# Last key block and corner of an attention output: from plain fp32 products to rounded ones, with the probabilities' way through DRAM cut in four

## The chip, the core and the metric

The kernel runs on one core of a Trainium2 chip. The metric is the device time of one execution in microseconds, as the median of the runs shown. The profile is of one execution by itself; it says when each instruction of each engine began and how long it took. The engines are TensorE (PE, with its weight loads listed apart as PEld), VectorE (DVE), ScalarE (ACT), GpSimd (POOL), and SyncE (SP), which here issues nearly all DMAs. L605 is line 605 of the kernel.

## What is computed

Causal attention with a decay for 4 x 8 heads of 576 tokens and 64 columns, then two MLPs over all 2304 tokens.

```python
def _attn_ref(q, k, v, f):                      # (4, 8, 576, 64)
    scores = scale * np.matmul(q, k.transpose(0, 1, 3, 2))
    log_f = np.log(np.clip(f, 0.0001, 1.0))
    cum = np.cumsum(log_f, axis=-1)
    decay = cum[:, :, :, None] - cum[:, :, None, :]
    scores = np.where(causal, -1000000000.0, scores + decay)
    ...
    attn = attn / (np.sum(attn, axis=-1, keepdims=True) + 1e-09)
    return np.matmul(attn, v)

x = attn_out.transpose(0, 2, 1, 3).reshape(2304, 512)
h = np.maximum(x @ w_in, 0.0);  x = (h * h) @ w_out
h = x @ w_in2;                  out = (h - np.tanh(h)) @ w_out2
```

## The kernel before

**Rounded products.** TensorE multiplies the type F32R in one pass, and plain F32 in two (the profile lists 32 instructions for the 16 products of L602). Where precision matters, the kernel splits a number into a rounded high part and the rest as a low part (`rounded`, `rest`) and adds up three products: high x high, low x high, high x low. The first MLP does so for each of its tiles of 288 tokens (`hp` at L164, `yp` at L193, twelve products of a step in a row), and so do the scores (`s_ps`).

**Stages.** Heads 0 to 7 run first, their second half beside the first MLP tile. Heads 8 to 15, here the early heads, run beside tiles 0 and 1 in pieces that `attention` issues. Heads 16 to 31, the late heads, run beside tiles 2 to 5: `plan_head` puts each step of a head into a numbered half step of the MLP, 7.75 of them from one head to the next. Behind them come the last two tiles and the second MLP. Each engine's instructions stand in one order: that of a first build up to tile 2, and the order in which the code emits them from there.

**One head.** The scores go through a row minimum (DVE, L497), an exponential (ACT, L506) and a division by the sum (POOL, L517). The probabilities `P[t]` must then be turned, keys to partitions. Early heads turn them on PE (`trans`, bank `t_ps`), where ACT rounds the high part into `PTh` and DVE writes the low part to `PTl`. Late heads turn them in 32x32 pieces on DVE (`turn`, into `T`), and the pieces get to their partitions by way of DRAM: `put` stores the whole of `T` in one DMA to `p_d`, `get` reads it back into `PTl` in four, one for each set of 32 partitions. In the next head's slots ACT rounds `PTl` to `PTh` in four steps, one per key block (`p_high`), and DVE leaves the rest in `PTl` (`p_low`).

**The output of a head** (`pv_parts`). `o_ps` holds 64 columns of V's high part times the probabilities in its lower half and V's low part in its upper half: the weights `VH[:, c]` have both, 128 columns. A product per key block and part of the probabilities: `(hi, 0)` to `(hi, 3)` and `(lo, 0)` to `(lo, 3)`. I call the first group of a late head its high block (`pv_begin`), the second its low block (`pv_end`); an MLP step stands between. Two pieces are plain F32, with raw V as weights (`VR`): the last key block of 64 keys, which only the last 128 queries see (`po4`, L602), and the corner, the first 64 queries with their own 64 keys (`corner`, L609, into a bank of its own).

```python
seq = [(hi, 0), (hi, 1), (hi, 2), (hi, 3), (None, 4), (lo, 1), (lo, 2), (lo, 3), (lo, 0)]
...
nc.tensor.matmul(po4, vr[0:rows, 4], p4, start=False, stop=False)
```

In a late head the 64 keys of the last block and the corner lie in places of `T` that causality leaves free: column block 2, piece 0, and column block 3, piece 0. They pass through `PTl` without being rounded.

**The queue on SP.** It goes in order; an instruction that waits holds up all behind it. In a late head: `put`, in every second head the two stores of x (`x_d`, L489 and L490), `get`, then the loads of the next queries and keys (`R`, `QB`) and of V (`VR`, two buffers).

## Time and profile before

| | |
|---|---|
| median of 3 runs | 1013.88 us (1013.79 to 1014.28) |
| the profiled execution | 1015.15 us, of which the span of the program is 1013.4 |
| PE busy | 990.9 us, 98% |
| weight loads (PEld) | 930.6 us, 92% |
| DVE, ACT, POOL busy | 706.9, 608.6, 381.3 us (70%, 60%, 38%) |
| heads 8 to 15 | about 140 to 253 us of the span |
| heads 16 to 31 | about 253 to 523 us |

Busy time of PE is to be read with care: a product counts as busy from its start to its modelled end, overlaps with the next one, and counts on while it stands for an operand. What a product takes from PE's time is the distance from its start to the next one's.

### The profile page before, as it was taken

What the parts mean: (1) busy time and instruction counts of PE and PEld (TensorE: products, weight loads), DVE (VectorE), ACT (ScalarE), POOL (GpSimd) and SP (SyncE); (2) the same over time, 40 slices, a digit from 0 to 9 for tenths busy, and PEclk for the clock granted to TensorE, in tenths of its full rate; (3) what the DMA queues carried; (4) which work ended last, traced back from release to release, by engine and by line L of the source; (5) the groups of instructions that cost most, each with busy time, mean ns of one, the idle gap of its engine ahead of it and who ended that gap; (6) DMA issues with size and microseconds to landing.
All of it is one profiled execution on the core that took longest, in us unless ns stands there. A gap on an engine that the chain in (4) does not pass through costs nothing.

```text
span 1013.4 us, 19745 instructions
## 1 busy us (share of the span) xinstructions
PE 990.9 (98%) x7120; PEld 930.6 (92%) x7120; DVE 706.9 (70%) x1675; ACT 608.6 (60%) x1347; POOL 381.3 (38%) x453
## 2 busy tenths in 40 slices
PE   7979999999999999999999999999999999999998
PEld 7767678888999899998999999999999999999998
DVE  5886675777676777675825668477777787877851
ACT  4886676766776667676746777456556553333330
POOL 3453455555543324343402456247456520000000
PEclk8999999999999999999999999999999999999999
DMA  8545542223556556665547984997776699434451
GB/s 265 233 139 189 182 155 81 98 80 112 213 217 230 203 209 208 224 219 187 196 150 250 357 290 172 367 381 254 282 271 249 235 343 343 147 118 135 139 167 63
DMA packets 84529, 211.54 MB, mean 209 GB/s; under 512 B 8440, under 2 KB 33072, under 8 KB 80080
## 3 DMA queue, kind: packets, MB, share of 16 engines
q1 hardware_dynamic: 84304, 210.28, 59.2%
q8 instruction: 56, 0.92, 0.4%
q14 instruction: 41, 0.34, 0.1%
q10 hardware_dynamic: 128, 0.01, 0.0%
HBM read 132.20 MB, written 78.05 MB: 207 GB/s over the span
## 4 chain that ended last, share of the span: by engine, by line
PE 77%; DMA 8%; DVE 6%; ACT 3%; issue 2%; POOL 2%; SPq 1%; DVEq 0%; ACTq 0%; POOLq 0%
PE yp L193 17%; PE hp L164 17%; PE wp L1270 16%; PE wp L1194 11%; PE o_ps L605 4%; PE wp L1282 2%; DMA raw<-in_w_dram 2%; DMA R<-in_qk_dram 2%; DMA g_d<-gq 2%; PE o_ps L406 1%; DMA PTl<-p_d 1%; DVE wt L966 1%; PE s_ps L698 1%; PE t_ps L541 1%; PE s_ps L697 1%
## 5 line engine op out<-in xcount | busy, mean ns | idle before, releaser
L164 PE MATMUL hp<-xhl,w 128*128 128x288 f32 x1536 | 236.3, 299 | 2.5 <-POOL xhl L122 1.0
L164 PEld LDWEIGHTS hp<-xhl,w 128*128 128x128 f32 x1536 | 213.1, 189 | 7.8 <-issue 1.8
L193 PE MATMUL yp<-gh,w 128*128 128x288 f32 x1024 | 212.8, 299 | 0.0
L193 PEld LDWEIGHTS yp<-gh,w 128*128 128x128 f32 x1024 | 164.4, 188 | 3.1 <-issue 2.1
L1194 PE MATMUL wp<-xo,wg 128*128 128x288 f32 x1152 | 159.9, 296 | 2.0 <-DVE gq L1201 1.9
L1270 PE MATMUL wp<-go,wg 128*128 128x256 f32 x1344 | 161.4, 283 | 0.0
L1270 PEld LDWEIGHTS wp<-go,wg 128*128 128x128 f32 x1344 | 161.4, 192 | 0.0
L1194 PEld LDWEIGHTS wp<-xo,wg 128*128 128x128 f32 x1152 | 155.0, 188 | 3.5 <-DVE gq L1201 3.4
L193 PE MATMUL yp<-gl,w 128*128 128x288 f32 x512 | 151.5, 297 | 0.0
L517 POOL TENSOR_SCALAR P<-P,ST 128x448 f32<-128x448 f32 (+4 forms) x120 | 83.4, 704 | 136.6 <-DVE ST L713 83.0
L109 ACT ACTIVATE go<-gt 128x1792 fp32r<-128x1792 f32 (+1 forms) x34 | 58.3, 1717 | 101.2 <-PE wp L1270 79.9
L497 DVE CUSTOM_DVE_ANT_0 P<-s_ps,mk 128x320 f32<-128x320 f32 (+3 forms) x151 | 63.5, 438 | 72.6 <-PE s_ps L698 41.5
L506 ACT ACTIVATE P<-P,ST 128x320 f32<-128x320 f32 (+4 forms) x151 | 84.8, 562 | 47.3 <-DVE ST L497 45.2
L193 PEld LDWEIGHTS yp<-gl,w 128*128 128x128 f32 x512 | 96.4, 188 | 0.8 <-issue 0.8
L122 DVE TENSOR_TENSOR gl<-tmp,gh 128x288 fp32r<-128x288 f32 x96 | 58.6, 611 | 51.6 <-ACT tmp L174 51.1
L122 DVE TENSOR_TENSOR go<-gt,go 128x1792 fp32r<-128x1792 f32 (+1 forms) x34 | 69.6, 2048 | 34.9 <-ACT go L109 32.0
L170 ACT ACTIVATE tmp<-hp 128x288 f32<-128x288 f32 x128 | 52.0, 406 | 63.1 <-PE hp L164 62.2
L122 POOL TENSOR_TENSOR wt<-wt,whi 128x512 f32<-128x512 f32 (+1 forms) x48 | 60.7, 1286 | 59.2 <-ACT whi L109 28.8
L174 ACT ACTIVATE tmp<-tmp 128x288 f32<-128x288 f32 x128 | 56.7, 443 | 3.4
L173 ACT ACTIVATE gh<-tmp 128x288 fp32r<-128x288 f32 x128 | 56.1, 438 | 1.9
L1201 DVE TENSOR_TENSOR gq<-wp,sm 128x288 f32<-128x288 f32 x96 | 40.8, 453 | 17.0 <-ACT sm L1200 11.3
L1245 DVE TENSOR_TENSOR gt<-gt 128x256 f32<-128x256 f32 x128 | 49.4, 428 | 1.5 <-DMA gt<-g_d 0.4
(171 smaller groups left out, 1673.7 us busy)
## 6 DMA issues: line engine op xcount, KB each, us to landing
wg<-wg_d SPq DMA_DIRECT2D x24, 896.0 KB
g_d<-gq SPq DMA_DIRECT2D x32, 576.0 KB
raw<-in_w_dram SPq DMA_DIRECT2D x16, 1024.0 KB
p_d<-T SPq DMA_DIRECT2D x16, 1024.0 KB
PTl<-p_d SPq DMA_DIRECT2D x64, 256.0 KB
raw<-in_w_dram SPq DMA_DIRECT2D x32, 512.0 KB
gt<-g_d SPq DMA_DIRECT2D x32, 512.0 KB
R<-in_qk_dram SPq DMA_DIRECT2D x24, 576.0 KB
```

The source lines that it names most:

```text
L109: eng.activation(out, in_, AF.Copy)
L122: eng.tensor_tensor(out, in_, hi.bitcast(F32), ALU.subtract)
L164: nc.tensor.matmul(ps, w[:, k * 128:(k + 1) * 128], x[:, k], start=(jj == 0), stop=(jj == 11))
L170: nc.scalar.activation(tmp, ps, AF.Relu)
L173: nc.scalar.activation(gh, tmp, AF.Square)
L174: nc.scalar.activation(tmp, tmp, AF.Square)
L193: nc.tensor.matmul(yp[m][:, :n], w[:, c], x, start=(at == 0 and j == 0), stop=(at == NF - 1 and j == 2))
L497: nc.vector.tensor_tensor_reduce(p[:rows, a:b], ps[:rows, :b - a], mk[:rows, o:o + b - a], -0.125, 3.0e38 if mn is None else mn, ALU.add, ...
L506: nc.scalar.activation(p[:rows, :n], p[:rows, :n], AF.Exp, bias=mn, scale=-1.0, accum_out=st[:rows, 1, t:t + 1])
L517: by(n_by).tensor_scalar(p[:rows, :n], p[:rows, :n], st[:rows, 3, t:t + 1], 1.0, ALU.mult, ALU.mult)
L1194: nc.tensor.matmul(ps, wg[:, ws, k * 128:(k + 1) * 128], xo[:, xs, k], start=(i == 0 and first_), stop=(i == 5), skip_group_check=True)
L1270: nc.tensor.matmul(ps, wg[:, ws, m * 128:(m + 1) * 128], YO[n][xs][:, YX[xn]], start=(j == 0 and m == 0 and i == 0), stop=(j == 2 and i == ...
```

## The change

The last key block becomes two rounded products, `(hi, 4)` and `(lo, 4)`, and the corner three (high x high, V's low part x high, high x low). For that V's fifth block is rounded too (`VH` has 5 blocks, and `VR` is only read by that rounding, so it has one buffer; the load of V moves behind the rounding in `attention`). The pieces of probabilities that lay in `PTl` raw are now split as well: `p_high(2)`, `p_low(2)` start at piece 0 and `p_high(3)`, `p_low(3)` at piece 1 instead of 2 (`LOW`). In early heads two DVE copies out of `t_ps` become one ACT and one DVE step of 64x192. `put` becomes four stores of a quarter each; each of the loads of `get` reads one quarter. `get` moves one half step ahead, from o + 7 to behind o + 6, and so ahead of the x stores. Left out of the diff: every second one of heads 0 to 7 keeps its V in the buffer of `VH`, since `VR` has one buffer now, and the table of engines (the new ACT step `pth3` as `pth` before).

```diff
@@ -62,6 +62,7 @@
 DIRECT = ((0, 6), (0, 7), (1, 6), (1, 7))
 HOME_G = {6: 0, 7: 1, 0: 2, 1: 3, 2: 4, 3: 5, 4: 6, 5: 7}
 YSEQ = (0, 6, 1, 7, 2, 3, 4, 5)
+LOW = (0, 0, 0, 1)
 PT_SZ = (64, 256, 384, 512, 576)
 
 
...
@@ -285,14 +286,15 @@
         by(pre(u) + "st").memset(ST[u], 1.0)
 
     def load_v(u):
-        VR[u] = two.tile([128, 5, D], F32, tag="VR", bufs=2, name="VR")
+        VR[u] = two.tile([128, 5, D], F32, tag="VR", bufs=1, name="VR")
         src = v[u] if u < UT else v[u].rearrange("(b i) c d -> i b (c d)", b=4)
         nc.sync.dma_start(VR[u], src)
 
     def prep_v(u):
-        VH[u] = one.tile([128, 4, 2, D], F32R, tag="VH", name="VH")
-        rounded(by(pre(u) + "vh"), VH[u][:, :, 0], VR[u][:, 0:4])
-        rest(by(pre(u) + "vl"), VH[u][:, :, 1], VR[u][:, 0:4], VH[u][:, :, 0])
+        VH[u] = one.tile([128, 5, 2, D], F32R, tag="VH", name="VH")
+        vr = VR.pop(u)
+        rounded(by(pre(u) + "vh"), VH[u][:, :, 0], vr)
+        rest(by(pre(u) + "vl"), VH[u][:, :, 1], vr, VH[u][:, :, 0])
 
 
     A_RAW, A_V, A_QA, A_QB = {}, {}, {}, {}
...
@@ -546,15 +551,14 @@
         rounded(nc.scalar, PTh[:, :nch, t - 1], src)
         rest(nc.vector, PTl[:, :nch, t - 1], src, PTh[:, :nch, t - 1])
         if t == 1:
-            rounded(by("ptr"), PT["t"][0:64, :, 3, 1], ps[0:64, 256:384].rearrange("p (q j) -> p q j", q=4))
-            rounded(by("ptr"), PT["t"][0:64, 2:4, 3, 0], ps[0:64, 384:448].rearrange("p (q j) -> p q j", q=2))
-
-
+            eh, el = (x[0:64, 3].rearrange("p t j -> p (t j)")[:, :192] for x in (PTh, PTl))
+            rounded(nc.scalar, eh, ps[0:64, 256:448])
+            rest(nc.vector, el, ps[0:64, 256:448], eh)
 
     def turn(t):
         p, T = P[t], PT["t"]
         if t == 0:
-            nc.vector.transpose(T[0:64, 0:2, 3, 0], p[0:64, :64].rearrange("p (b j) -> p b j", b=2))
+            nc.vector.transpose(T[0:64, 0:2, 3, 1], p[0:64, :64].rearrange("p (b j) -> p b j", b=2))
             return
         nch = min(t + 1, 4)
         nc.vector.transpose(T[:, :, :nch, t - 1].rearrange("p b a j -> p a b j"),
...
@@ -563,7 +567,8 @@
             nc.vector.transpose(T[:, 0:2, 2, 0], p[:, 512:576].rearrange("p (b j) -> p b j", b=2))
 
     def put(u):
-        by("put").dma_start(p_d[u % 2], PT["t"].rearrange("p b a s j -> p (b a s j)"))
+        for b in range(4):
+            by("put").dma_start(p_d[u % 2][:, 512 * b:512 * b + 512], PT["t"][:, b].rearrange("p a s j -> p (a s j)"))
 
     def get(u):
         src = p_d[u % 2].rearrange("(q i) (b n) -> i q b n", q=4, b=4)
...
@@ -572,41 +577,38 @@
             by("get").dma_start(dst.bitcast(F32), src[:, :, b])
 
     def pv_parts(u):
-        vh, vr = VH.pop(u), VR.pop(u)
+        vh = VH.pop(u)
         b, h = divmod(u, H)
         e = h % 2
         ps = bank(u, "o_ps")
         if u < UT:
             hi, lo = (PT[k].rearrange("p q a s j -> p (q a s j)").rearrange("p (c t j) -> p c t j", c=4, t=4) for k in "hl")
             po = ps.rearrange("p (s j) -> p s j", s=4)
-            at = lambda p, c, t: p[:, c, t:]
+            at = lambda p, c, t: p[0:64, 3, 0] if c == 4 else p[:, c, t:]
+            po_at = lambda t: po[:, t:]
+            p0 = lambda p: p[0:64, 3, 1, :64]
             rows = 64
-            po4, p4 = ps[0:64, 384:512].rearrange("p (q j) -> p q j", q=4), PT["t"][0:64, :, 3, 1]
-            po_at = lambda t: po[:, t:]
-            p0 = PT["t"][0:64, 2:4, 3, 0]
+            seq = [(hi, 0), (hi, 1), (lo, 1), (hi, 2), (lo, 2), (hi, 4), (hi, 3), (lo, 3), (lo, 4), (lo, 0)]
         else:
             hi, lo = PT["h"], PT["l"]
             po = ps.rearrange("p (q s j) -> p q s j", q=4, s=4)
-            at = lambda p, c, t: p[:, :, c, t:]
+            at = lambda p, c, t: p[:, :, 2, 0] if c == 4 else p[:, :, c, t:]
+            po_at = lambda t: po[:, :, t:]
+            p0 = lambda p: p[:, 0:2, 3, 1]
             rows = 128
-            po4, p4 = po[0:64, :, 3], lo[:, :, 2, 0].bitcast(F32)
-            po_at = lambda t: po[:, :, t:]
-            p0 = lo[:, 0:2, 3, 0].bitcast(F32)
-        seq = [(hi, 0), (hi, 1), (lo, 1), (hi, 2), (lo, 2), (hi, 3), (lo, 3), (None, 4), (lo, 0)]
-        if u >= UT:
-            seq = [(hi, 0), (hi, 1), (hi, 2), (hi, 3), (None, 4), (lo, 1), (lo, 2), (lo, 3), (lo, 0)]
+            seq = [(hi, 0), (hi, 1), (hi, 2), (hi, 3), (hi, 4), (lo, 1), (lo, 2), (lo, 3), (lo, 4), (lo, 0)]
+        po4 = po[:, 3] if u < UT else po[:, :, 3]
 
         def products(a, z):
             for n, (pt, c) in list(enumerate(seq))[a:z]:
-                if pt is None:
-                    nc.tensor.matmul(po4, vr[0:rows, 4], p4, start=False, stop=False)
-                    continue
                 t = max(0, c - 1)
-                nc.tensor.matmul(po_at(t), vh[:, c].rearrange("p a d -> p (a d)"), at(pt, c, t), start=(n == 0), stop=(n == 8))
+                w, o = (vh[0:rows, c], po4) if c == 4 else (vh[:, c], po_at(t))
+                nc.tensor.matmul(o, w.rearrange("p a d -> p (a d)"), at(pt, c, t), start=(n == 0), stop=(n == len(seq) - 1))
 
         def corner():
             ps0 = PS0[u] = bank(u, "o0_ps")
-            nc.tensor.matmul(ps0[0:64, 0:64], vr[0:rows, 0], p0, start=True, stop=True)
+            for n, (a, p) in enumerate(((0, hi), (1, hi), (0, lo))):
+                nc.tensor.matmul(ps0[0:64, 0:64], vh[0:rows, 0, a], p0(p), start=(n == 0), stop=(n == 2))
 
         xt = one.tile([64, 512], F32, tag="xsh", name="xt")
 
...
@@ -636,7 +638,7 @@
 
     def pv(u):
         products, corner, upper, out = pv_parts(u)
-        products(0, 9)
+        products(0, 10)
         corner()
         upper()
         out()
...
@@ -653,8 +655,6 @@
 
     def attention(u0):
         for p in range(u0 - 2, UT):
-            if u0 - 1 <= p:
-                load_v(p + 1)
             for t in (1, 4, 3, 2):
                 if p >= u0:
                     trans(p, t)
...
@@ -670,12 +670,13 @@
                     prep(p + 2)
                 if t == 3 and p >= u0:
                     prep_v(p)
+                if t == 3 and u0 - 1 <= p:
+                    load_v(p + 1)
             if p + 3 < NU:
                 load(p + 3)
             if p >= u0:
                 pv(p)
             if p + 1 == UT:
-                nc.gpsimd.memset(PT["t"][0:64, 2:4, 3, 0], 0.0)
                 turn(1)
                 turn(0)
                 put(UT)
...
@@ -716,11 +717,11 @@
         normalise(P[t], ST[u], t, f"{pre(u)}n{t}")
 
     def p_high(c):
-        s0 = max(0, c - 1)
-        rounded(by("pth"), PT["h"][:, :, c, s0:], PT["l"][:, :, c, s0:].bitcast(F32))
+        s0 = LOW[c]
+        rounded(by("pth3" if c == 3 else "pth"), PT["h"][:, :, c, s0:], PT["l"][:, :, c, s0:].bitcast(F32))
 
     def p_low(c):
-        s0 = max(0, c - 1)
+        s0 = LOW[c]
         lo = PT["l"][:, :, c, s0:]
         rest(by(f"ptl{c}"), lo, lo.bitcast(F32), PT["h"][:, :, c, s0:])
 
...
@@ -745,7 +746,7 @@
         PV[u][0](0, 5)
 
     def pv_end(u):
-        PV[u][0](5, 9)
+        PV[u][0](5, 10)
         PV[u][1]()
 
     def plan(slot, f, *a, behind=False):
...
@@ -795,7 +796,7 @@
             plan(o + 5, turn, 1)
             plan(o + 5, turn, 0)
             plan(o + 5, put, k)
-            plan(o + 7, get, k)
+            plan(o + 6, get, k, behind=True)
         if k == UT + 1:
             plan(o, prep_v, UT)
         if k + 1 < NU:
```

The products of late head 18 on **PE**, `o_ps<-PTh` the high block and `o_ps<-PTl` the low block, with the MLP step (`yp`) between. Before:

```order
L605 MATMUL o_ps<-PTh,VH 128x512 x2
L605 MATMUL o_ps<-PTh,VH 128x4x96
L605 MATMUL o_ps<-PTh,VH 128x4x64
L602 MATMUL o_ps<-PTl,VR 64x4x32
...
L605 MATMUL o_ps<-PTl,VH 128x512
L605 MATMUL o_ps<-PTl,VH 128x4x96
L605 MATMUL o_ps<-PTl,VH 128x4x64
L605 MATMUL o_ps<-PTl,VH 128x512
L609 MATMUL o_ps<-PTl,VR 64x64
```

and with the change (its lines are 1 or more further down):

```order
L606 MATMUL o_ps<-PTh,VH 128x512 x2
L606 MATMUL o_ps<-PTh,VH 128x4x96
L606 MATMUL o_ps<-PTh,VH 128x4x64
L606 MATMUL o_ps<-PTh,VH 128x4x32
...
L606 MATMUL o_ps<-PTl,VH 128x512
L606 MATMUL o_ps<-PTl,VH 128x4x96
L606 MATMUL o_ps<-PTl,VH 128x4x64
L606 MATMUL o_ps<-PTl,VH 128x4x32
L606 MATMUL o_ps<-PTl,VH 128x512
L611 MATMUL o_ps<-PTh,VH 64x64 x2
L611 MATMUL o_ps<-PTl,VH 64x64
```

The rows that read `VR` (F32, 64 columns of weights, each two passes on the chip) are gone; one product over 4x32 columns stands at the end of the high block and one in the low block, and three of 64 columns behind the low block.

The same stretch of heads on the **SP queue**, two heads in a row, the first with x stores behind its predecessor's output. Before:

```order
L566 DMA p_d_83<-T 128x2048
L489 DMA x_d_81<-xsh 128x576
L490 DMA x_d_81<-xs 128x576
L572 DMA PTl<-p_d_83 32x4x512 x4
L269 DMA R<-in_qk_dram 128x1152
L271 DMA QB<-aug_d 4x1152
L290 DMA VR<-in_v_dram 128x1x320
L566 DMA p_d_84<-T 128x2048
L572 DMA PTl<-p_d_84 32x4x512 x4
```

and with the change:

```order
L571 DMA p_d_83<-T 128x512 x4
L577 DMA PTl<-p_d_83 32x4x512 x4
L494 DMA x_d_81<-xsh 128x576
L495 DMA x_d_81<-xs 128x576
L270 DMA R<-in_qk_dram 128x1152
L272 DMA QB<-aug_d 4x1152
L291 DMA VR<-in_v_dram 128x1x320
L571 DMA p_d_84<-T 128x512 x4
L577 DMA PTl<-p_d_84 32x4x512 x4
```

One store of 2048 columns became four of 512, and the four loads stand right behind them, ahead of the two x stores; the loads of R, QB and VR kept their places behind.

## Rows read from the trace of the kernel before

**Rows 1.** The page: busy time of each engine and its share of the span.

```profile
PE 990.9 (98%) x7120; PEld 930.6 (92%) x7120; DVE 706.9 (70%) x1675; ACT 608.6 (60%) x1347; POOL 381.3 (38%) x453
```

**Rows 2.** Waits of PE: engine, line, releaser: total us, times, longest.

```profile
PE o_ps L605 <- issue: 0.9, 1, 0.9
```

**Rows 3.** Timeline of PE, head 16: start us, us, engine, line, operation.

```profile
266.40 0.91 PE L605 MATMUL o_ps<-PTh,VH 128*128 128x512 f32 x4
267.24 0.43 PE L602 MATMUL o_ps<-PTl,VR 128*64 128x128 f32 x2
267.60 1.85 PE L164 MATMUL hp<-xhl,w 128*128 128x288 f32 x12
269.29 0.92 PE L605 MATMUL o_ps<-PTl,VH 128*128 128x512 f32 x4
270.13 0.33 PE L609 MATMUL o_ps<-PTl,VR 128*64 128x64 f32 x2
270.39 0.53 PE L193 MATMUL yp<-gh,w 128*128 128x288 f32 x2
270.76 0.30 PE L193 MATMUL yp<-gl,w 128*128 128x288 f32 x1
```

**Rows 4.** The same timeline, twelve MLP products with rounded products around them.

```profile
259.05 1.75 PE L164 MATMUL hp<-xhl,w 128*128 128x288 f32 x12
260.64 0.31 PE L697 MATMUL s_ps<-QA 128*128 128x320 f32 x1
```

**Rows 5.** Timeline of PE, an early head.

```profile
224.87 0.28 PE L605 MATMUL o_ps<-PTh,VH 128*128 128x256 f32 x1
224.99 0.28 PE L605 MATMUL o_ps<-PTl,VH 128*128 128x256 f32 x1
225.20 0.43 PE L602 MATMUL o_ps<-T,VR 64*64 64x128 f32 x2
225.56 0.50 PE L605 MATMUL o_ps<-PTl,VH 128*128 128x512 f32 x1
```

**Rows 6.** Timeline of PE, rounded score products over 64 columns.

```profile
261.13 0.21 PE L697 MATMUL s_ps<-QA 128*128 128x64 f32 x1
261.18 0.28 PE L698 MATMUL s_ps<-QB 68*128 68x64 f32 x1
```

**Rows 7.** Timeline of the weight loads beside them.

```profile
261.04 0.19 PEld L697 LDWEIGHTS s_ps<-QA 128*128 128x128 f32 x1
261.16 0.19 PEld L698 LDWEIGHTS s_ps<-QB 68*128 68x128 f32 x1
```

**Rows 8.** Timeline of the SP queue: stores and loads of turned probabilities.

```profile
318.31 0.33 SPq L566 DMA_DIRECT2D p_d<-T  x1
...
324.25 2.54 SPq L572 DMA_DIRECT2D PTl<-p_d  x4
...
335.88 0.32 SPq L566 DMA_DIRECT2D p_d<-T  x1
340.06 2.53 SPq L572 DMA_DIRECT2D PTl<-p_d  x4
```

**Rows 9.** Lines by form, ScalarE: busy us, mean ns, idle before and releaser.

```profile
L109 ACT ACTIVATE PTh<-PTl 128x512 fp32r<-128x512 f32 x32 | 18.4, 623 | 16.7 <-DMA PTl<-p_d 16.7
...
L109 ACT ACTIVATE PTh<-PTl 128x256 fp32r<-128x256 f32 x16 | 6.4, 403 | 0.0
```

**Rows 10.** Timeline of ScalarE, one head: idle before in brackets.

```profile
348.17 1.87 ACT L109 ACTIVATE PTh<-PTl 128x512 fp32r<-128x512 f32 x4 [1.47 <-DMA PTl<-p_d]
```

**Rows 11.** Busy time of the instructions on o_ps in 16 windows, one per high block.

```profile
266.00:268.60 2.60, 1.27 (x6) 0.89 (x6) 0.00 (x0) 0.00 (x0) 1.00 0.07 25
...
348.50:351.80 3.30, 1.89 (x6) 0.94 (x6) 0.00 (x0) 0.00 (x0) 1.00 0.47 170
...
sum 48.30, PE 24.97 PEld 14.61 DVE 0.00 ACT 0.00; mean PE 1.56 PEld 0.91 DVE 0.00 ACT 0.00
```

**Rows 12.** Busy time of all engines, clock, DMA share and GB/s, one stretch.

```profile
319.00:321.50 2.50, 2.50 (x18) 2.14 (x17) 1.58 (x3) 1.06 (x3) 2.10 (x3) 1.00 1.01 413
```

More of the change, by code (lines that the diff above doesn't have):

```diff
@@ L330, in first @@
             r = (one if tag == "R" else two).tile([128, 2, S], F32, tag=tag, name="R0")
-            vr = two.tile([128, 5, D], F32, tag="VR", bufs=2, name="VR")
+            if h % 2:
+                vr = one.tile([128, 5, 2, D], F32, tag="VH", name="V0").rearrange("p c a d -> p (c a d)")[:, :5 * D].rearrange("p (c d) -> p c d", c=5)
+            else:
+                vr = two.tile([128, 5, D], F32, tag="VR", bufs=1, name="VR")
             nc.sync.dma_start(r[0:64], qk[h][0:64])
```

2 rows, old and new, of the table ENG are left out of this document.

## The prediction

> **What bounds the kernel now.** I read the page's engine line first: TensorE (PE) is busy for 98% of the span, and the weight loads for 92% [rows 1]. So a microsecond of PE work that goes away is a microsecond of time, wherever PE isn't standing for somebody else. The list of PE's waits holds little, 0.9 us as its largest before the attention's last products [rows 2], but a product that stands for its operand counts as busy, so busy time hides the rest. The timeline of PE by start times therefore decides: the distance from one start to the next is what a product costs.
>
> **The late heads (16 to 31).** In one of them [rows 3] PE runs four rounded products on the high parts (266.40), two passes of the plain fp32 product of the last key block (267.24), one step of the MLP, four rounded products on the low parts (269.29), two passes of the plain fp32 corner (270.13), and goes on. The fp32 block takes 267.24 to 267.60 = 0.36 us, the corner 270.13 to 270.39 = 0.26 us. Around them lies a second cost, which the durations don't tell. The twelve products behind the fp32 block take 267.60 to 269.29 = 1.69 us, where twelve undisturbed ones take 259.05 to 260.64 = 1.59 us [rows 4]: 0.10 us to leave fp32. Likewise the two products behind the corner take 270.39 to 270.76 = 0.37 us against 2 x 0.133 = 0.27: 0.10 again. Entering costs about as much: in an early head [rows 5] one product over 256 columns takes 0.12 us (224.87 to 224.99) and the next one, alike but with fp32 behind it, 0.21 (to 225.20): 0.09 us. There the fp32 block takes 225.20 to 225.56, the same 0.36.
>
> So each head pays for the block 0.09 + 0.36 + 0.10 = 0.55 us and for the corner 0.09 + 0.26 + 0.10 = 0.45, together **1.00 us**; I take the early heads' exits and corner as the late ones'.
>
> **What takes their place on PE.** Five rounded products: high and low part of the last block (128 columns of probabilities, 128 of weights) and three corner products (64 and 64). No such product is in the trace. The nearest rows are the rounded score products over 64 columns [rows 6]: from one to the next 0.05 us. But the weight loads beside them, of 128 columns, start 0.12 us apart [rows 7], so a stream of such products goes at the pace of its loads. I price a product by the load it must leave room for: 0.11 where the next load has 128 columns (between the 0.12 here and the 0.10 that the exposed first load costs behind fp32), and half, 0.06, where it has 64, an estimate. Late heads: 0.11 + 0.11 + 0.06 + 0.06 + 0.11 = 0.45; early heads, where the third corner product stands apart: 0.11 + 0.11 + 0.06 + 0.11 + 0.11 = 0.50. Net per head: 0.55 (16 late ones) and 0.50 (8 early ones): 8.8 + 4.0 = **12.8 us** off PE. Bounds: all five at 0.05 gives 0.75 x 24 = 18.0; all five at the 0.133 of a product over 288 columns gives (1.00 - 0.665) x 24 = 8.0. I stay near the middle, since the loads' row is of the nearest shape.
>
> The Trainium skill (TensorE: Matmul & The Clock Gate, LDWEIGHTS) puts a weight load at its columns over 1.2, which is 107 ns for 128 columns and 53 for 64: the trace's 0.12 agrees, and no row here shows the other alone. The same page (Back-to-back issue gap) gives about 81 ns for a load and product of 128 columns in a stream; by that the two wide products would be 0.03 us cheaper each, an estimate of 24 x 0.06 = 1.4 us more gain.
>
> **The store and load of turned probabilities.** A late head's probabilities go out as one store of 1 MB and come back as four loads. Without attention stores in between, the loads stand from 335.88 to 340.06 for the store to land, 4.18 us; in every second head the two x stores stand ahead of them, and they go out at 324.25, 5.9 us after the store of 318.31 [rows 8]. They land late: ScalarE stands idle for them for 16.7 us in all [rows 9]. In one head it waits 1.47 us, goes at 348.17 into the four rounding steps [rows 10], and PE follows product by product. The table of PE's time in the 16 high blocks [rows 11] sums that up: an undisturbed one has 1.27 us, the one behind 348.17 has 1.89, and eight of the 16 have 1.67 or more. Sixteen undisturbed ones would have 20.3, the sum is 24.97: 4.6 us of standing inside the blocks, and the 0.9 of [rows 2] ahead of one of them. Together **5.5 us**.
>
> After the change the loads need only their own quarter, and PTl free (PE's corner of the head before). The whole store's data flow for the 2.5 us from 319.0 to 321.5 [rows 12]; a quarter has 0.6, so the first should land 4.18 - 1.9 = 2.3 us after its issue, and the others follow about as fast as the loads can be issued (0.63 each). Loads start 1.9 us earlier in the heads without stores and, standing ahead of the stores now, 3.6 earlier in the others. The head at 348.17 waited 1.47, so it is covered. ScalarE's rounding gets longer: pieces of 384 and 256 columns become 512 and 384, together 623 - 403 = 0.22 us per head [rows 9], and the low parts on VectorE by about as much. Where the loads are early this lies under the MLP step ahead of the block; if that cover is gone it costs 0.22 x 16 = 3.5 us. I count 5.0 of the 5.5 us as won. Ends: nothing, and 5.5.
>
> **Other edits.** In the early heads two VectorE copies become one ScalarE and one VectorE step of 64x192, and V's fifth block is rounded too. ScalarE's nearest row is 0.40 us [rows 9]; PE reads these late in its block, so MLP products hide it; shown uncovered it would be 0.40 x 8 = 3.2 us. I charge 0.5. One V buffer less: the load of V now stands behind the rounding of the V before, on the SP queue ahead of the query/key load R; a head is 17 us long (318.31 to 335.88), V is needed one head later, so I charge nothing. Behind the earlier loads wait the x stores, by at most 4 x 0.63 = 2.5 us, and they feed an MLP tile that comes much later. The part before the early heads and all behind the last head keep their order.
>
> **Sum.** -12.8 - 5.0 + 0.5 = -17.3 us. The profiled execution took 1015.15 us (span 1013.4 and 1.75 around it), 1.27 above the median of 1013.88. 1015.15 - 17.3 = 997.85, less 1.27: **996.6 us**.
>
> **Rivals.**
> - *The stalls stay* (18%). The quarters or PTl's release hold the loads back, or ScalarE comes late for its own reasons. For it: PE gets faster, so each load has less time. Against it: 1.9 and 3.6 us of lead. 996.6 + 5.0 = 1001.6.
> - *The small products are dear* (12%): 0.133 each. 996.6 + 4.8 = 1001.4. For it: none of this shape is in the trace. Against: 0.05 at 64 columns.
> - *The freed PE time is swallowed* (6%): VectorE and ScalarE, both longer now, set the pace in part; half of 12.8 is lost: 1003.0. Against: they are busy for 70% and 60% [rows 1].
> - *Slower: the four quarter stores land one after the other* (4%). If each paid the whole store's time but for its data, 4.18 - 1.9 = 2.3 us in turn, the last lands after 9.2. The last load now goes out at 340.06 + 1.9 = 341.96; then at 335.88 + 9.2 = 345.1, 3.1 us later, and in the other heads at 327.5 instead of 326.1, 1.4 later. 8 x 3.1 + 8 x 1.4 = 36 us of lateness; the 8 heads without a stall today can hide perhaps 1.5 each (my choice), 12, so 24 us are added: 1013.88 - 12.3 + 24 = 1025.6. It decides once the lateness beyond that cover passes 12.3 us, about 1.5 us in each head. For it: the four loads of a quarter take from 340.06 to 348.17, 8.1 us, twice as long as the whole store. Against: the store alone fills the DMA engines at 413 GB/s [rows 12], and nothing in the rows makes one quarter wait for another. The Trainium skill (DMA: Bandwidth & Descriptors, Rules for kernel authors) speaks for this rival: coalesce small transfers, 1 MiB and more for bandwidth, since each has a fixed part of about 2.0 us. By the page's fit a quarter takes 2.6 us, an estimate; four in turn would be 10.4, and no row shows whether they go in turn.
> - *No change worth measuring* (3%): the time between PE's parts is filled again.
>
> **How the numbers follow.** The forecast's own case has 57%. The rivals that still gain (36%) lie at 1001 to 1003; the lower end is both terms at their best, 1013.88 - 18.0 - 5.5 + 0.5 = 990.9. The range 990 to 1003 leaves out the slower and the neutral case and what is beyond the bounds. Faster by over 0.2% (2 us, about what can be told here): 0.93; within it: 0.03; slower: 0.04.
>
> **What would show it.** On PE: no fp32 passes in heads 8 to 31, five short products of 0.05 to 0.13 us, and no 0.1 us loss behind them. The 16 high blocks, now five products each: near 0.95 us plus the drain, without the stalled half. On SP: the first load some 2.3 us after the first quarter store. On ScalarE: the 16.7 us of waiting for PTl down to a few. It is wrong if PE's distances between starts shrink and the time doesn't, or if ScalarE still stands for PTl.

## The result

The changed kernel takes 1004.42 us (median of 4 runs, 1003.81 to 1005.74), the kernel before 1014.08 beside it (4 runs, 1013.79 to 1015.37): a ratio of 0.9904, 95% interval 0.9887 to 0.9921. The profiled execution took 1004.15 us, its span is 1002.4, so 11.0 less than before where 17.3 were forecast. PE's busy time on the page is 979.8 us, 11.1 less than in [rows 1], and by itself that says nothing about where. Three marks cut the span: PE's 64x64 turn, which each of the early heads 8 to 15 has once, the start of head 16's high block, and the first product of the second MLP.

**The early heads lost time.** PE's 64x64 transposes, before and after (of each group: duration, then start of its first and last):

```profile
L544 PE MATMUL t_ps<-ident,P x8: 242/243/244, 143.9 to 240.6; 64*64 64x64 f32 x8
```

```profile
L549 PE MATMUL t_ps<-ident,P x8: 242/243/244, 142.9 to 242.0; 64*64 64x64 f32 x8
```

From the first to the last of the eight, seven heads, it was 96.7 us and is 99.1 now: 2.4 longer. Head 16's high block starts at 269.00, where before it was 266.40 [rows 3]: 2.6 later, and 3.5 earlier was forecast.

**The late heads gained what was forecast.** PE's timeline in head 16, as [rows 3] had it (start, length, instructions):

```profile
269.00 0.98 PE L606 MATMUL o_ps<-PTh,VH 128*128 128x512 f32 x5
269.82 1.81 PE L165 MATMUL hp<-xhl,w 128*128 128x288 f32 x12
271.46 1.03 PE L606 MATMUL o_ps<-PTl,VH 128*128 128x512 f32 x5
272.33 0.25 PE L611 MATMUL o_ps<-PTh,VH 128*64 128x64 f32 x2
...
272.47 0.51 PE L194 MATMUL yp<-gh,w 128*128 128x288 f32 x2
272.82 0.30 PE L194 MATMUL yp<-gl,w 128*128 128x288 f32 x1
```

The fp32 pieces are gone. The four high products with the fp32 block, and the twelve MLP products behind it, took 266.40 to 269.29 = 2.89 us; the five high products and the same twelve take 269.00 to 271.46 = 2.46; the low ones, the corner and the two MLP products behind it took 269.29 to 270.76 = 1.47 and take 271.46 to 272.82 = 1.36. That is 0.54 us a head, and 0.55 was forecast.

The stalls in the high blocks are gone too, but for one (the 16 windows, as [rows 11]):

```profile
268.60:270.40 1.80, 0.98 (x5) 0.87 (x5) 0.00 (x0) 0.00 (x0) 1.00 0.00 0
...
347.50:350.00 2.50, 1.54 (x5) 0.86 (x5) 0.00 (x0) 0.00 (x0) 1.00 0.43 155
...
sum 27.80, PE 16.24 PEld 13.98 DVE 0.00 ACT 0.00; mean PE 1.01 PEld 0.87 DVE 0.00 ACT 0.00
```

Undisturbed blocks have 0.97 to 0.99, the one of head 21 has 1.54: the sum is 0.6 over 16 times 0.98, where before it was 4.6 over. ScalarE's wait for the low tile fell from the 16.7 us of [rows 9] to 1.8:

```profile
L110 ACT ACTIVATE PTh<-PTl 128x512 fp32r<-128x512 f32 x48 | 26.6, 621 | 2.8 <-DMA PTl<-p_d 1.8 <-issue 1.0
```

The SP queue, as [rows 8], shows why (start, us, instructions):

```profile
270.40 1.79 SPq L571 DMA_DIRECT2D p_d<-T  x4
272.71 2.97 SPq L577 DMA_DIRECT2D PTl<-p_d  x4
...
318.77 2.48 SPq L571 DMA_DIRECT2D p_d<-T  x4
321.45 2.99 SPq L577 DMA_DIRECT2D PTl<-p_d  x4
324.49 0.58 SPq L494 DMA_DIRECT2D x_d<-xsh  x1
```

The first load goes out 2.31 us after the first quarter store (270.40 to 272.71), and 2.68 in the other head shown, where 2.3 was forecast; over the late heads it is 2.2 to 3.6, mostly 2.2 to 2.3. The x stores now stand behind the four loads (324.49).

**Behind attention** nothing changed. The first rounded product of the second MLP and the first of its last part (L1194 and L1270 before, one line lower after), before and after:

```profile
L1270 PE MATMUL wp<-go,wg x1344: 280/283/283, 825.2 to 986.3; 128*128 128x256 f32 x192
L1194 PE MATMUL wp<-xo,wg x1152: 288/294/402, 642.9 to 824.2; 128*128 128x288 f32 x192
```

```profile
L1271 PE MATMUL wp<-go,wg x1344: 280/283/284, 814.2 to 975.3; 128*128 128x256 f32 x192
L1195 PE MATMUL wp<-xo,wg x1152: 288/294/403, 632.1 to 813.2; 128*128 128x288 f32 x192
```

It starts at 632.1 in place of 642.9, and takes 182.1 us to its last part in place of 182.3. The balance: +2.6 to head 16, then 363.1 us to the second MLP in place of 376.5, -13.4, and -0.2 behind it: -11.0, the difference of the spans.

### The profile page after: what moved, and what is told of

It reads as the page before. It is cut to its first block, busy times and chain, and to the rows that moved or that the text cites. A ratio compares the mean times of both kernels' runs of the same rounds, so it can differ in the third digit from the quotient of the medians.

```text
span 1002.4 us, 19872 instructions
## 1 busy us (share of the span) xinstructions
PE 979.8 (98%) x7144; PEld 931.6 (93%) x7144; DVE 717.1 (72%) x1667; ACT 612.4 (61%) x1355; POOL 393.1 (39%) x452
## 4 chain that ended last, share of the span: by engine, by line
PE 80%; DVE 7%; DMA 5%; ACT 3%; issue 2%; POOL 1%; SPq 1%; DVEq 0%; POOLq 0%; ACTq 0%
PE hp L165 18%; PE yp L194 17%; PE wp L1271 16%; PE wp L1195 13%; PE o_ps L606 4%; PE wp L1283 2%; PE o_ps L411 2%; DMA raw<-in_w_dram 1%; DVE wt L967 1%; PE s_ps L699 1%; DMA g_d<-gq 1%; PE t_ps L546 1%; PE s_ps L698 1%; PE t_ps L392 1%; DVE P L502 1%
## 5 line engine op out<-in xcount | busy, mean ns | idle before, releaser
L522 POOL TENSOR_SCALAR P<-P,ST 128x448 f32<-128x448 f32 (+4 forms) x120 | 93.9, 790 | 137.8 <-DVE ST L714 77.5
L1333 POOL TENSOR_TENSOR gq<-sm,sm 128x288 f32<-128x288 f32 x32 | 28.5, 892 | 55.7 <-ACT sm L1332 34.6
```

Source lines behind the costliest of these rows:

```text
L522: by(n_by).tensor_scalar(p[:rows, :n], p[:rows, :n], st[:rows, 3, t:t + 1], 1.0, ALU.mult, ALU.mult)
```

## The experiments

The table holds all of them, as the text below reads them. "Early" is the time from the first to the last of the eight turns, "late" from head 16's high block to the second MLP, "second MLP" as above; these three are from one profiled execution each, the ratio from the timed ones. Each ratio is to the kernel before as it was timed beside that row's kernel; its medians there lay between 1014.08 and 1015.51 us, so medians of different rows can differ by a microsecond or two for that reason alone.

| kernel | median us (range; runs) | ratio to before, 95% | early | late | second MLP |
|---|---|---|---|---|---|
| before | 1013.88 (1013.79 to 1014.28; 3) | | 96.7 | 376.5 | 182.3 |
| after | 1004.42 (1003.81 to 1005.74; 4) | 0.9904 (0.9887 to 0.9921) | 99.1 | 363.1 | 182.1 |
| after, again | 1006.82 (1005.08 to 1008.06; 6) | 0.9909 (0.9875 to 0.9942) | 99.2 | 362.5 | 185.2 |
| 128 rows | 1004.06 (999.38 to 1006.26; 4) | 0.9889 (0.9857 to 0.9921) | 94.6 | 363.1 | 185.2 |
| 128 rows, again | 1003.29 (999.46 to 1005.56; 6) | 0.9869 (0.9835 to 0.9903) | 94.3 | 362.1 | 183.3 |
| adjacent | 1005.48 (1001.2 to 1008.56; 4) | 0.9906 (0.9874 to 0.9939) | 97.4 | 363.0 | 184.6 |
| 128 rows for the turn too | 1002.6 (999.1 to 1006.45; 5) | 0.9869 (0.9846 to 0.9892) | 94.9 | 362.0 | 187.0 |
| late heads on 64 rows | 1020.95 (1018.19 to 1027.24; 8) | 1.0047 (1.002 to 1.0075) | 100.8 | 376.8 | 185.9 |
| late part only | 1005.85 (1003.46 to 1009.49; 6) | 0.9903 (0.9869 to 0.9937) | 98.8 | 362.3 | 183.8 |
| products alone | 1016.58 (1012.88 to 1021.29; 10) | 1.0022 (1.0003 to 1.0042) | 98.6 | 372.9 | 186.1 |
| transfers alone | 1013.01 (1007.82 to 1015.7; 10) | 0.9961 (0.9931 to 0.9991) | 97.2 | 370.4 | 185.6 |
| whole store, early loads | 1008.03 (1005.13 to 1013.67; 10) | 0.9935 (0.9909 to 0.9962) | 99.2 | 366.2 | 182.6 |
| quarters, late loads | 1011.15 (1008.13 to 1014.78; 10) | 0.9962 (0.9945 to 0.9979) | 99.2 | 369.5 | 182.3 |

**How to read it.** The second MLP takes 182.1 to 187.0 us from one execution to another, with no order by kernel. Its largest group of waits on PE, in after and in the same kernel once more (total, times, longest):

```profile
PE wp L1195 <- DVE gq L1202: 1.6, 2, 1.4
```

```profile
PE wp L1195 <- DVE gq L1202: 3.6, 5, 1.7
```

So two medians some 3 us apart can hardly be told apart. The stretches are steadier: of the six executions with the early heads of after, five have 98.6 to 99.2 us for them (the sixth 100.8), and the late stretch of a kernel profiled twice differs by 0.6 and 1.0. I read those, and the medians where they agree.

### What the early heads lost

In after, one early head on PE, and behind it the same stretch of the kernel before:

```profile
197.77 0.73 PE L606 MATMUL o_ps<-PTh,VH 128*128 128x512 f32 x2
198.43 0.30 PE L611 MATMUL o_ps<-PTh,VH 64*64 64x64 f32 x2
...
198.72 0.40 PE L165 MATMUL hp<-xhl,w 128*128 128x288 f32 x1
...
199.19 0.34 PE L606 MATMUL o_ps<-PTh,VH 128*128 128x384 f32 x1
199.38 0.34 PE L606 MATMUL o_ps<-PTl,VH 128*128 128x384 f32 x1
199.65 0.64 PE L606 MATMUL o_ps<-PTh,VH 64*128 64x128 f32 x2
200.12 0.96 PE L606 MATMUL o_ps<-PTl,VH 128*128 128x256 f32 x3
200.92 0.55 PE L165 MATMUL hp<-xhl,w 128*128 128x288 f32 x3
```

```profile
197.04 0.73 PE L605 MATMUL o_ps<-PTh,VH 128*128 128x512 f32 x2
...
197.96 0.67 PE L164 MATMUL hp<-xhl,w 128*128 128x288 f32 x3
...
200.07 1.09 PE L164 MATMUL hp<-xhl,w 128*128 128x288 f32 x7
```

From the first product to the end of the block it takes 197.77 to 200.92 = 3.15 us with one MLP product inside; before it was 197.04 to 200.07 = 3.03 with three. Less 0.133 for each of these: 3.02 against 2.63. The head has lost 0.39 us, where the forecast had 0.50 won; read in the same way, the eight early heads lose 0.37 to 0.58 each. In the rows of after the products with `64*128` and `64*64` stand out. The one over 384 columns ahead of the first takes 199.38 to 199.65 = 0.27 (its neighbour, alike but with 128 rows behind it, 0.19); and 199.65 to 200.12, a 64-row product and one over 256 columns, is 0.47.

**Theory:** a product over 64 rows between products over 128 rows costs TensorE a switch on the way in and one on the way out. **Rivals:** the products stand for operands that come late; a narrow product is dear by itself; the V buffers.

**128 rows.** The early heads' small products over all 128 rows; rows 64 to 127 of the probabilities are zeros, written once, so the result stays.

```diff
-            at = lambda p, c, t: p[0:64, 3, 0] if c == 4 else p[:, c, t:]
-            p0 = lambda p: p[0:64, 3, 1, :64]
-            rows = 64
+            at = lambda p, c, t: p[:, 3, 0] if c == 4 else p[:, c, t:]
+            p0 = lambda p: p[:, 3, 1, :64]
+            rows = 128
```

Expected:

> The changed kernel, but the early heads' last-block and corner products run over 128 rows in place of 64 (rows 64 to 127 of the probabilities are zeros written once, so the result is the same). Theory (a product over 64 rows between products over 128 rows costs TensorE about 0.1 us on the way in and 0.1 on the way out, as the trace of after has it: 0.45 for each of two, and about 0.49 for the corner): each last-block product falls to about 0.11 to 0.12 and the corner to about 0.23, 0.9 us a head over 8 heads, so 1004.4 - 7 = 997.5 us (996 to 999.5). Rival 1 (the products stand for probabilities that ScalarE and VectorE round late): no change, 1004.4, and the products keep 0.25 us. Rival 2 (a product over 128 columns alone among wider ones is dear whatever its rows): no change, 1004.4. Rival 3 (the loss sits in the loads of V): no change on the whole, though the products become cheap.

And timed once more, beside the changed kernel itself:

> The changed kernel once more, beside its variants on one chip. Both theories: 1004.4 us by the runs so far; the executions of the kernel before spread from 1012.5 to 1017.7 on this chip, so the median here may lie 1 to 2 us away from it. The stretch of the early heads, from the first MLP products of head 8's steady part to those of head 16, should again be longer than in the kernel before, by 1 to 2 us.

> The changed kernel with the early heads' last-block and corner products over 128 rows, timed beside the changed kernel itself. In its first look PE reached the end of the early heads 5.1 us earlier than in the changed kernel, and 4.1 us of that stood at the end of attention. Theory (the row switch is what the early heads lost by): 4 us below the changed kernel of the same call, 1000.4 if that stands at 1004.4. Rival (the last projection fills the time again, by a wait of its own): within 1 us of the changed kernel.

The same head of the second of them:

```profile
195.84 0.73 PE L606 MATMUL o_ps<-PTh,VH 128*128 128x512 f32 x2
196.41 0.25 PE L611 MATMUL o_ps<-PTh,VH 128*64 128x64 f32 x2
...
196.56 0.38 PE L165 MATMUL hp<-xhl,w 128*128 128x288 f32 x1
...
197.29 0.34 PE L606 MATMUL o_ps<-PTl,VH 128*128 128x384 f32 x1
197.47 0.39 PE L606 MATMUL o_ps<-PTh,VH 128*128 128x128 f32 x2
197.70 0.63 PE L606 MATMUL o_ps<-PTl,VH 128*128 128x256 f32 x3
198.16 0.55 PE L165 MATMUL hp<-xhl,w 128*128 128x288 f32 x3
```

The product over 384 columns takes 197.29 to 197.47 = 0.18 now, the two behind it 0.23 in place of 0.47, the three low ones 197.70 to 198.16 = 0.46 in place of 0.80 (200.12 to 200.92), the corner 196.41 to 196.56 = 0.15 in place of 0.29. The stretch is 2.32 us: 0.83 less than in after, with the same number of products over the same columns, and 0.44 less than before once the MLP products are taken off (0.50 was forecast). The transfers, the rounding steps and the one V buffer are those of after, and the products have the same columns: so it isn't operands, narrowness or the V buffer. "Early" falls by 4.5 and 4.9 us to below that of before. Timed side by side, the medians differ by 3.5 us, where 4 was expected; the first timing's 1004.06 lies outside the 996 to 999.5 expected of it. So not all of the gain arrives. Seven times 0.83 would be 5.8 in "early", and there PE's wait for a bank that VectorE's output step frees grows from 1.3 us in after to 2.2 in the first execution with 128 rows (1.9 in the second). Behind the early heads PE also stands longer for an MLP tile that comes from DRAM, 1.70 us where it was 0.67 in after:

```profile
262.70 0.76 PE L165 MATMUL hp<-xhl,w 128*128 128x288 f32 x3 [1.70 <-DMA xhl<-x_d]
```

**Adjacent.** The two 64-row products one behind the other.

```diff
-            seq = [(hi, 0), (hi, 1), (lo, 1), (hi, 2), (lo, 2), (hi, 4), (hi, 3), (lo, 3), (lo, 4), (lo, 0)]
+            seq = [(hi, 0), (hi, 1), (lo, 1), (hi, 2), (lo, 2), (hi, 3), (lo, 3), (hi, 4), (lo, 4), (lo, 0)]
```

Expected:

> The changed kernel, but in the early heads the two 64-row products of the last block stand one behind the other in place of two 128-row products apart. Theory (the switch between 64 and 128 rows is paid at each way in and out): one way in and one way out fewer, 0.19 us a head, so 8 x 0.19 = 1.5 us less: 1002.9 (1002 to 1003.6). Rival 1 (operands late): the earlier of the two moves behind two more products and the later stays, so no change or up to 0.5 less. Rival 2 (each narrow product dear by itself): no change, 1004.4.

The same head of it:

```profile
197.45 0.73 PE L606 MATMUL o_ps<-PTh,VH 128*128 128x512 f32 x2
...
200.25 0.42 PE L165 MATMUL hp<-xhl,w 128*128 128x288 f32 x2
```

It takes 2.80 us with one MLP product inside, 0.35 less than in after: more than the 0.19 of the theory, and neither rival has room for it. "Early" falls by 1.7 to 1.8 us, where seven times 0.19 would be 1.3; the median can't tell it from after.

**Late heads on 64 rows.** The reverse: a switch where there was none. This kernel leaves the keys in the other 64 rows out.

```diff
-            at = lambda p, c, t: p[:, :, 2, 0] if c == 4 else p[:, :, c, t:]
-            p0 = lambda p: p[:, 0:2, 3, 1]
-            rows = 128
+            at = lambda p, c, t: p[0:64, :, 2, 0] if c == 4 else p[:, :, c, t:]
+            p0 = lambda p: p[0:64, 0:2, 3, 1]
+            rows = 64
```

Expected:

> The changed kernel, but the late heads' last-block and corner products run over 64 rows in place of 128: the keys in rows 64 to 127 of that block and corner are left out of the late heads' sums. Same columns, same number of products, same transfers. Theory (the way into 64 rows and out of them costs TensorE about 0.1 us each, and the last-block product with it 0.45 in place of 0.11): 0.34 more for each of two products and 0.26 for the corner, 0.94 us in each of 16 heads, so 15 us more: 1019.5 to 1022 (1016 if the low products come late and hide some). Rival (what is dear in the early heads is their place among short products, or operands that come late): no change, 1004.4 to 1006.8, and the starts in the late blocks stay 0.11 and 0.23 us apart.

One late head of it, around its high and its low block:

```profile
342.23 1.18 PE L606 MATMUL o_ps<-PTh,VH 128*128 128x512 f32 x5
343.34 0.53 PE L194 MATMUL yp<-gh,w 128*128 128x288 f32 x2
...
345.04 1.38 PE L606 MATMUL o_ps<-PTl,VH 128*128 128x512 f32 x5
346.35 0.30 PE L611 MATMUL o_ps<-PTh,VH 64*64 64x64 f32 x2
...
346.64 0.53 PE L165 MATMUL hp<-xhl,w 128*128 128x288 f32 x2
```

The high block takes 342.23 to 343.34 = 1.11 in place of 0.82, the low one 1.31 in place of 0.87, the corner 346.35 to 346.64 = 0.29 in place of 0.14: 0.88 together, beside what the exits cost the MLP products behind them. "Late" grows by 13.7 to 14.3 us, and the medians, from different timings, by 14 to 16.5; 15 was expected. This and the 128 rows settle it: the price goes with the rows, in both directions.

**128 rows for the turn too.** Does it hold for other products?

```diff
-            nc.tensor.transpose(ps[0:64, 384:448], P[0][0:64, :], ident[0:64, 0:64])
+            nc.tensor.transpose(ps[0:64, 384:512], P[0], ident)
```

Expected:

> The kernel with 128 rows in the early heads' last-block and corner products, and one step more: the last turn of each early head on PE, 64x64, runs over 128 rows too (the rows added are zeros, so the result is the same). In the trace with 128-row products the turn ahead of it takes 0.204 us to the next start, where its neighbours take 0.109, and the turn itself 0.173. Theory (any product over 64 rows between others pays for the switch, transposes too): both fall to about 0.11, 0.16 us a head, so 1.3 us in 8 heads, to 1002 by the median of 1003.3 measured for the kernel without this step; that is less than the spread of its executions, so the starts around the turn decide. Rival (it is the rounded products alone, or their high and low order): the two starts keep their 0.20 and 0.17.

One such turn in this kernel, and behind it one in the kernel without this step:

```profile
201.04 0.27 PE L548 MATMUL t_ps<-ident,P 128*64 128x128 f32 x1
...
201.18 0.34 PE L535 MATMUL s_ps<-QA 128*128 128x192 f32 x1
```

```profile
199.55 0.27 PE L548 MATMUL t_ps<-ident,P 128*64 128x128 f32 x1
...
199.93 0.36 PE L535 MATMUL s_ps<-QA 128*128 128x192 f32 x1
```

From the fp32 turn ahead of it to the score product behind it, it takes 201.04 to 201.18 = 0.14 us now, where in the kernel without this step it was 199.55 to 199.93 = 0.38. So the switch shows at a transpose too. But "early" doesn't get shorter: PE waits instead for the bank that VectorE's output step frees (first this kernel, then the one without the step; total, times, longest):

```profile
PE s_ps L535 <- DVE xs L624: 4.3, 5, 1.2
```

```profile
PE s_ps L535 <- DVE xs L624: 2.1, 4, 1.0
```

The 2.2 us more of it, by one execution each, are about what 8 x 0.24 should have brought. By this releaser the early heads have come to a second limit, the end of a head on VectorE.

**Late part only.** The early heads' fp32 products put back, with one V buffer as in after, and with them the load of V moved behind the last product that reads raw V. Of the edit, the move:

```diff
-                if t == 3 and u0 - 1 <= p:
-                    load_v(p + 1)
             if p >= u0:
                 pv(p)
+            if u0 - 1 <= p:
+                load_v(p + 1)
```

Expected:

> The changed kernel with the early heads' products put back: their last block and corner are plain fp32 products over 64 rows again, with the load of V behind them; the late heads are as in the changed kernel. Theory (in the early heads rounded products over 64 rows cost more than the fp32 ones that they replace): the early heads take 1.5 us less than in the changed kernel, 1002.9 (1001.5 to 1004). Rival (the rounded products gain there too and the loss is the V buffer's or the start's): 3.5 us more, 1007.9.

By the times it can't be read. The late load of V makes a wait of its own (VectorE stands for it, and ScalarE's rounding behind that), 1.7 us in all ahead of the first product of three heads. "Early" is 98.8 with these waits in it; the median is 1.0 us under that of after, within the noise, and above the 1001.5 to 1004 that was expected. What PE does from a head's first product on can be read:

```profile
195.43 0.73 PE L611 MATMUL o_ps<-PTh,VH 128*128 128x512 f32 x2 [0.62 <-ACT PTh L110]
...
196.35 0.67 PE L165 MATMUL hp<-xhl,w 128*128 128x288 f32 x3
...
198.46 0.43 PE L165 MATMUL hp<-xhl,w 128*128 128x288 f32 x2
```

195.43 to 198.46 = 3.03 us with three MLP products inside is what it was before (197.04 to 200.07), with the one V buffer of after. So the head's loss came with the products, not with the buffer.

### What the transfers brought

**Products alone.** The whole store, and the loads back in their slot.

```diff
-        for b in range(4):
-            by("put").dma_start(p_d[u % 2][:, 512 * b:512 * b + 512], PT["t"][:, b].rearrange("p a s j -> p (a s j)"))
+        by("put").dma_start(p_d[u % 2], PT["t"].rearrange("p b a s j -> p (b a s j)"))
...
-            plan(o + 6, get, k, behind=True)
+            plan(o + 7, get, k)
```

Expected:

> The changed kernel with one whole store of the turned probabilities and the loads one slot later, as before: the product change alone. Theory (the stalls of the late high blocks went through the earlier loads): ScalarE again waits for the low tile, some 16 us in all or more, and the time rises by the 5 us that the prediction gave to this edit, to 1009.5 (1008 to 1011). Rival (the stalls went because the products changed, and the transfers are hidden anyway): 1004.4.

**Transfers alone.** The opposite two edits on the kernel before. Expected:

> The kernel before with the transfer edit alone: the four quarter stores, and the loads one slot earlier, ahead of the x stores; all products, V buffers and rounding steps as before. The prediction gave this edit 5.0 us. Theory (the stalls were 5.5 us and go): 5 us under the kernel before of the same call, ScalarE's waiting for the low tile falls from 16.7 us to a few. The two edits then don't add up: 5 alone, but 8 behind the new products. Rival (the loads that go out earlier hold up the x stores or something else): less than 2 us under, or nothing.

ScalarE's first rounding group, products alone and transfers alone (busy us, mean ns, idle before and releaser):

```profile
L110 ACT ACTIVATE PTh<-PTl 128x512 fp32r<-128x512 f32 x48 | 26.8, 621 | 20.6 <-DMA PTl<-p_d 20.5
```

```profile
L109 ACT ACTIVATE PTh<-PTl 128x512 fp32r<-128x512 f32 x32 | 18.3, 622 | 1.0 <-issue 1.0
```

Against the 376.5 us of before, the late stretch takes 3.6 less with the products alone, 6.1 less with the transfers alone, and 13.4 to 14.0 less with both. The edits don't add up: 9.7 by themselves. As whole kernels, products alone is no faster than before (ratio 1.0022, and 1016.58 where 1008 to 1011 was expected), since its early heads lose what after's lose, and transfers alone is 2.5 us under the kernel before beside it, where 5 was expected; the second MLP, 186.1 and 185.6 us in these two executions, blurs both. With the old transfers, ScalarE's wait for the low tile grows from 16.7 to 20.5 us, and PE stands for it: from start to start, its products of the 16 high blocks take 21.8 us with the products alone and 15.0 in after, where in the kernel before it was 18.1, and 13.6 with the transfers alone. So PE comes to each high block sooner and waits there for loads that come no sooner, issued 3.9 to 6.2 us behind their store in both kernels with the old transfers: of the 8.8 us that the products were to free, 3.6 arrive. With the transfers alone no wait for the low tile is left (the 1.0 listed is "issue"), with both edits 1.8 us, and behind the new transfers the products bring 7.3 to 7.9 us of late stretch (370.4 to 363.1 and 362.5).

**Each transfer edit by itself**, on the new products: the whole store with the early loads, and the quarters with the late ones. Expected:

> The changed kernel with one whole store in place of four quarters, its loads still one slot earlier and ahead of the x stores. With both undone PE stood 8.7 us longer by the end of attention, with only the place of the loads undone 7.1. Theory (the place of the loads is what counts, the quarters little): 1.6 to 3 us over the changed kernel, 1006 to 1007.5. Rival (each edit needs the other: a load that comes early only waits for the whole store): near the products alone, 7 to 9 us over, 1012 to 1013.

> The changed kernel with the four quarter stores kept and the loads one slot later, behind the x stores, as before. Theory (in the heads with x stores the loads are held by their place in the queue, in the others by the store): the quarters alone win the heads without stores, so about half of the 5 us comes back as stalls: 1007 (1005.5 to 1008.5). Rival (a quarter's early landing is all that matters): 1004.4.

From the 372.9 us of the products alone, the loads' earlier place takes off 6.7 and the quarters 3.4; both together take off 9.8. So the place counts twice as much, and neither needs the other. Against after, the quarters are worth 3.1 us of the stretch, and 1.2 by the medians timed side by side, which is within the noise; 1.6 to 3 was expected. With the place undone, the median of 1011.15 lies above the 1005.5 to 1008.5 expected, and the stretch is 6.4 longer than in after.

## Why the prediction was wrong

The forecast was 996.6 us, with 990 to 1003; it is 1004.42. By its steps:

- **Late heads, products: right.** Five new products priced at 0.45, and 0.46 found: 1.00 less the 0.54 won. Of the 0.10 behind each piece, which the forecast's signs had as gone, half or more stays: the twelve products behind the high block take 1.64 us (269.82 to 271.46) against 1.59, the two behind the corner 0.35 against 0.27. The price covers that, as room for the next load: the corner is 0.14 with 0.08 behind it, for which 0.23 was reckoned, and 0.24 is left for the wide two with what stands behind them, 0.12 each, the weight-load pace of [rows 7]. By the Trainium skill (TensorE: Matmul & The Clock Gate, Back-to-back issue gap), a stream with 128 columns goes at about 81 ns, so the wide two would have been 0.03 us cheaper each, about 0.08, an estimate. No run here has a stream of such products alone; the two here came at 0.12.
- **Early heads, products: this step failed.** "Early heads: 0.11 + 0.11 + 0.06 + 0.11 + 0.11 = 0.50", and from it "8 early heads: 4.0" off PE. These prices were taken from rows over 128 rows, [rows 6] and [rows 7], and put on products over 64. The five cost 1.00 + 0.39, about 1.4: 0.39 a head lost in place of 0.50 won. Over 128 rows the same products come out at -0.44, and the step would have stood, though the time still would not: that kernel takes 1003.3 to 1004.1, since part of what PE gains there goes into the waits for the bank and the MLP tile, and the second MLP of those executions took 1 to 3 us longer. The rows to see it were there: [rows 5] shows 0.09 ahead of the fp32 block, and its operands are `64*64`; I put all of that down to fp32 (which has a switch of its own: the late heads' blocks, over 128 rows, paid it too). The Trainium skill has a rule too (TensorEngine Tiling (Array Packing), Key Properties): "Mode switching requires drain", with the 64-row shapes among the modes it lists. The trace agrees that these cost a switch, with 0.08 to 0.09 us ahead of a 64-row product and more behind it; that it is a drain no run here shows, and the late corner over `128*64`, a shape that the Trainium skill lists too, shows no such price (0.14 us for three products, where over `64*64` it was 0.29). The prediction didn't weigh that rule, which speaks against 64-row products that stand apart.
- **Stalls, 5.0 of 5.5: right in size** (0.6 left of 4.6 inside the blocks), and the reason holds: first loads mostly 2.2 to 2.3 us behind their store, ahead of the x stores; the transfers alone took 6.1 off the late stretch. What the sum got wrong is the independence of its terms: by itself the products' term came to 3.6 and not 8.8. That the total for the late heads is right (13.4 against 13.8) rests on both edits being there.
- **Other edits, +0.5:** not to be told apart from the failed step; with 128 rows the early stretch is 2.1 to 2.4 us shorter than before, and 3.5 x 7 / 8 = 3.1 would be the forecast for it.
- **The balance** of the profiled execution: 6.3 us were missed, 6.1 of them ahead of head 16. The rest of the way to the median is the 1.27 us that I took off since the profiled execution of before lay above its median; that of after lies 0.27 below.
- **The rivals:** "the small products are dear" came nearest in kind, but named the wrong reason, their shape, and all 24 heads; 16 of them were priced right. "The stalls stay" is refuted by ScalarE's 1.8 us. "The four quarter stores land one after the other" is refuted by the loads: all four are out 5.3 us after the first store (270.40 to 275.68), and 5.7 in the other head shown, where that rival had the last quarter land after 9.2. The fixed 2.0 us and the fit that it took from the Trainium skill (DMA: Bandwidth & Descriptors, Anatomy of one DMA) stand there for DMAs that GpSimd issues, and these stores go out from SP. "The freed PE time is swallowed" lies nearest to the time measured, by luck: the late heads lost nothing to it in the changed kernel, and the early heads freed nothing.

## What to carry to other kernels

Price a product by a row with the same number of contraction rows and the same type, not the same columns alone: a 64-row product among 128-row ones costs about a third of a microsecond more, and zeros in the unused rows buy that back. Freed time on an engine that is waited for by its own feeders comes back only if the feeders get faster too: here the products alone brought 3.6 of 8.8 us in the late heads, and behind the new transfers 7.3 to 7.9. After removing a limit, look for the next wait before removing the same thing elsewhere, as the turn showed.

## What the hardware showed beyond that

- The switch between 64 and 128 rows isn't one of fp32 alone: rounded products pay it, 0.83 us a head in the early heads and 0.88 in the late ones, and around a transpose it shows as 0.38 us against 0.14. Score products over 68 rows don't: in [rows 6] they follow at 0.05.
- The second MLP's 182 to 187 us vary from execution to execution in every kernel; PE waits there for a VectorE tile (`gq`), 1.6 us in one and 3.6 in another execution of the same kernel. What makes that tile late stays open.
